# Loads ahead of stores in a step's DMA issues, and four output weights split in place instead of through DRAM

## The chip, the cores and the metric

One core of one Trainium2 chip runs the whole program. The metric is the device time of one execution in microseconds (us), the median of three runs. The profile is one more execution, recorded instruction by instruction.

## What is computed

```python
def _attn_ref(q, k, v, mem_k, mem_v):            # q, k, v: (4, 8, 768, 64)
    chunk, left_ctx, right_ctx = (32, 16, 8)
    for c in range(seq // chunk):                # queries c*32 to c*32+31
        k_full = [mem_k, k[l_start:r_end]]       # 8 memory rows and a local window
        a = softmax(q_c @ k_full.T / sqrt(64))
        out[c] = a @ v_full

def reference(...):
    x = attn_out as 3072 tokens x 512
    x = (sigmoid(x @ w_gate) * (x @ w_val)) @ w_out          # 512 -> 1536 -> 512
    h = x @ w_in                                             # 512 -> 2048
    g = (a0 + a1*h + a2*h**2 + a3*h**3) / (1 + |b0|*|h| + |b1|*h**2 + 1e-6)
    return g @ w_out                                         # 2048 -> 512
```

The first line of each function stands for its shapes; the window arithmetic is shortened. Weights arrive as 64-bit floats and are turned into 32-bit ones on the chip.

## The kernel before, in words

**Precision.** Each matrix operand is held as two parts, a high part (rounded to the type fp32r) and the rest, and each product is three matmuls (high by high, high by low, low by high). So a weight goes through four operations before it can be used. Two ACT passes (`conv_scale`, L309 and L310) and one DVE pass (`conv_bits`, L315) make a 32-bit tile from the 64-bit *stage tile* `st`. One ACT pass (`split_hi`, L344) and one DVE pass (`split_lo`, L348) make the pair of parts from that. A pair is a 128x2x512 tile named `wp` (first layer) or `wpw` (second layer).

**Weights through DRAM.** A pair that is needed again later is written to DRAM (`store_split`, L351, into `wqa`, `wqs` or `w2d`) and read back when needed (`load_split`, L354; `load_w2`, L996 to L1007, for the second layer's output weights in `w2d`). There are 32 units of second-layer weights. `need` lists them in the order in which they are wanted. The input weights of the second layer come first, on the whole, and its output weights last.

**Stages.** Tokens are taken in six blocks `j` of 512. (a) 24 steps, blocks 0 and 1 by 12 hidden tiles `f` (L919 to L935): gate and value products `gate_val` (L372), the sigmoid and its product, the output product `out1` (L574) of the step before, and parts of the attention (scores L112 and L219, the transposes L171 and L264, the products with v L186 and L279). Block 0 also converts the first layer's weights, three units a step. (b) `quads(2, ...)`, 12 steps: blocks 2 and 3 as one pair, with seven products in place of eight (L489). (c) `outs(3, ...)`, 13 steps: output products that are left of block 3, with attention for blocks 4 and 5 between them. (d) `quads(4, ...)`, 12 steps, and `outs(5, ...)`, 13 steps, the same for blocks 4 and 5. (e) The second layer, 6 blocks by 16 tiles (L617, L625 to L645, L656).

**What sets the order.** Nothing is scheduled by a planner. The text's order is each engine's order. A table `plan` holds calls for numbered steps (`at(step, fn, ...)`), and `run(fn, ...)` carries out those of the current step that have one of the names given. So the order of the `run` lines within a step sets the order on every engine. Nearly all transfers are issued by SP, one queue in program order. If one transfer there waits for the engine that makes its data, or for its buffer to come free, everything behind it waits as well. `STORES` (L917) are the writes of weight pairs, `LOADS` (L918) the reads of q, k, v and of stage tiles, and `store1_end` the writes of a finished block of the first layer (`x2d`, L595). Stage tiles and pairs share a pool of 20 buffers; a load waits until what last used its buffer has been read.

Of the kernel before, what the change touches and what calls it, by code (L numbers as in the profile page):

```python
# [22 lines left out]
NF1, NF2 = DFF1 // P, DFF2 // P  # L23
# [14 lines left out]
NPAIR = 8  # L38
PAIRS = ((2, 3), (4, 5))
AHEAD = 4  # L40


@with_exitstack
def fused_kernel(ctx: ExitStack, tc: tile.TileContext, q, k, v, w1, w2, coef, x2d, w2d, wqa, wqs, out):
# [267 lines left out]
    def conv_bits(key, dst):  # L312

        w0, y = words(key)
        nc.vector.scalar_tensor_tensor(  # L315
            out=dst.bitcast(I32), in0=y, scalar=3, in1=w0, op0=ALU.logical_shift_left, op1=ALU.bitwise_or
        )
        del stage[key]
# [20 lines left out]
    def split_tile(key):  # L339
        wp[key] = wpool.tile([P, 2, 512], F32R, tag="w", name="wp" + "_".join(map(str, key)))  # L340
        return wp[key]

    def split_hi(key, src):
        nc.scalar.activation(out=split_tile(key)[:, 0], in_=src, func=ACTF.Copy)  # L344

    def split_lo(key, src):
        t = wp[key]
        nc.vector.tensor_tensor(out=t[:, 1], in0=src, in1=t[:, 0].bitcast(F32), op=ALU.subtract)  # L348
# [4 lines left out]
    def load_split(key, src):  # L353
        nc.sync.dma_start(out=split_tile(key).bitcast(F32), in_=src)  # L354
# [9 lines left out]
    def b_tile(name, dt, shape):  # L364
        return bpool.tile(shape, dt, tag="b", name=name)
# [25 lines left out]
    def gate_val(j, f, m):  # L391
        if (j, f) == (0, 0):
            if m == 0:
                for u in range(2):
                    first[u] = ps(f"h0_0_{u}")
                for h in range(2):
                    for u in range(2):
                        gv_mm(first[u], j, f, u, h)
            gv_out(first[m], j, f, m)
            return  # L400
        pt = ps(f"h{j}_{f}_{m}")
        for h in range(2):
            gv_mm(pt, j, f, m, h)
        gv_out(pt, j, f, m)
# [63 lines left out]
    def quad_key(ja, fp, w):  # L468
        return ("q", ja, fp) + w

    def quad_load(ja, fp, i0=0, n=len(PRODUCTS)):
        for w, _, _ in PRODUCTS[i0 : i0 + n]:
            src = wqa[2 * fp + w[1], w[2]] if w[0] == "a" else wqs[4 * fp + w[1]]
            load_split(quad_key(ja, fp, w), src)

    def quad(ja, fp, m, fill):
# [6 lines left out]
        def product(i):  # L483
# [13 lines left out]
            if m == 1:  # L497
                del wp[quad_key(ja, fp, w)]
                if i < len(PRODUCTS) - AHEAD and fp < NF1 // 2 - 1:
                    quad_load(ja, fp + 1, i + AHEAD, 1)  # L500

# [48 lines left out]
    def g_held(j, f):  # L550
        key = j, f // 4
        if key not in gh:
            p, tag = (xpool, "x") if f < 8 else (bpool, "b")
            gh[key] = p.tile([P, 4, 512], F32, tag=tag, name=f"gh{j}_{f // 4}")
        return gh[key][:, f % 4]

    def g_split(key, sg, n):
        t = gpool.tile([P, 2, 512], F32R, tag="g", name="g" + "_".join(map(str, key)))
        nc.scalar.activation(out=t[:, 0, 0:n], in_=sg, func=ACTF.Copy)  # L559
        nc.vector.tensor_tensor(out=t[:, 1, 0:n], in0=sg, in1=t[:, 0, 0:n].bitcast(F32), op=ALU.subtract)  # L560
        gp[key] = t
# [3 lines left out]
    def out1(j, f, mid=None):  # L565

        if f == 0:
            acc[j] = [accp.tile([P, 512], F32, tag=f"acc{d}", name=f"acc{j}_{d}") for d in range(KT)]
        w, g = wp.pop((1, j, f, 2)), gp.pop((1, j, f))
        for d in range(KT):  # L570
            if d == 2 and mid:
                mid()
            for i, (a, b) in enumerate(TERMS):
                nc.tensor.matmul(  # L574
                    acc[j][d],
                    lhsT=w[:, a, d * P : (d + 1) * P],
                    rhs=g[:, b],
                    start=(f == 0 and i == 0),
                    stop=(f == NF1 - 1 and i == 2),
                )  # L580
        if f == NF1 - 1:
            store1(j)
# [10 lines left out]
    def store1_end():  # L593
        for j, d, s in held:
            nc.sync.dma_start(out=x2d[j, :, d], in_=s)  # L595
        held.clear()
# [126 lines left out]
    c2 = {}  # L723
# [7 lines left out]
    def conv2_bits(i):  # L731
        c2[i] = t2(f"c2_{i}")
        conv_bits(f"2_{i}", c2[i])

    def conv2_hi(i):
        split_hi(("w2", i), c2[i])

    def conv2_lo(i):
        split_lo(("w2", i), c2.pop(i))

    def conv2_store(i):
        store_split(("w2", i), w2d[i])
# [5 lines left out]
    def at(si, *call):  # L748
        plan.setdefault(si, []).append(call)
# [16 lines left out]
    for i in range(2 * NF1):  # L766
        s0 = 10 + i // 2
# [5 lines left out]
    for t in range(4, NPAIR, 2):  # L773
        s0 = 2 if t == 4 else 5
# [31 lines left out]
    S1 = len(steps)  # L806
# [6 lines left out]
    O1 = S1 + NF1  # L813
    Q2 = O1 + NF1 + 1
    O2 = Q2 + NF1
# [7 lines left out]

    need = sorted(range(2 * NF2), key=lambda u: u // 2 + 5 * (u % 2))
    conv_at = [4, 5, 7, 13, 15, 17, 19] + [S1 + 1 + i for i in range(5)] + [O1 + 1 + 3 * i for i in range(4)]
    rest = 2 * NF2 - len(conv_at)
    conv_at += [Q2 + i * 10 // rest for i in range(rest)]
    used = set()
    for u, s0 in zip(need, conv_at):
        at(s0, conv2_load, u, s0 not in used and (S1 <= s0 < O1 or s0 >= Q2))  # L830
        used.add(s0)
        at(s0 + 1, conv2, u)
        at(s0 + 1, conv2_bits, u)
        at(s0 + 2, conv2_hi, u)
        at(s0 + 2, conv2_lo, u)
        at(s0 + 3, conv2_store, u)

    PRE, LAG2 = 3, 5
    with tc.manual_schedule():
# [67 lines left out]
        def runner(si):  # L907
            acts = plan.get(si, [])

            def run(*fns):  # L910
                for fn, *args in acts:
                    if fn in fns:
                        fn(*args)

            return run

        STORES = conv2_store, w_comb_store, w1_store  # L917
        LOADS = load_qk, load_qk2, load_v, conv2_load, load_w1  # L918
        for si, (j, f) in enumerate(steps):  # L919
            run = runner(si)  # L920
            store1_end()
            run(*STORES)
            run(*LOADS)
            run(w1_load, quad_load)
            run(w1_hi, attn_exp, bits1)
            gate_val(j, f, 0)
            run(w1_lo, attn_sum, attn_mul, pv, attn_t, pair_t, w_comb, x_comb)
            gate_val(j, f, 1)
            run(scale1)
            g_split((1, j, f), sgs.pop((j, f)), 512)  # L930
            run(attn_qk, attn_max, conv2_hi, conv2, w_comb_hi, x_comb_hi)
            if si:
                out1(*steps[si - 1], mid=lambda: run(pair_out, pair_qk, pair_max))
            run(pair_sum)
            run(w_comb_lo, x_comb_lo, conv2_lo, conv2_bits)  # L935
# [4 lines left out]
        def load_out(n):  # L940
            nonlocal n_out
            for v in visits[n_out : n_out + n]:
                w1_load(*v, OUT)
            n_out += n

        def visit(run):
            nonlocal nv
            out1(*visits[nv], mid=lambda: run(pair_out, pair_qk, pair_max))
            nv += 1

        def quads(ja, s0, last):
            for i in range(NF1):
# [3 lines left out]
                if m == 0 and fp < NF1 // 2 - 1:  # L956
                    quad_load(ja, fp + 1, 0, AHEAD)
                if i:
# [12 lines left out]
        def outs(j, s0, fn):  # L971
            for i in range(NF1 + 1):
                run = runner(s0 + i)
                load_out(1)
                run(quad_load)
                store1_end()
                run(*STORES)
                run(*LOADS)
                for nxt in visits[nv + 2 : nv + 3]:
                    if nxt[0] == j:  # L980
                        g_split((1, *nxt), g_held(*nxt), 512)
                fn(i)
                run(x_comb, attn_exp)
                run(x_comb_hi, conv2_hi, conv2)
                visit(run)
                run(pair_t)
                run(x_comb_lo, conv2_lo, conv2_bits, pair_sum)

        quads(2, S1, False)
        outs(3, O1, lambda i: None)  # L990
        quads(4, Q2, True)
        nc.scalar.activation(out=cab, in_=cf[:, 4:6], func=ACTF.Abs)
        w2_next, w2t = 0, {}
        in_b = 14

        def load_w2(n):  # L996
            nonlocal w2_next
            for u in need[w2_next : w2_next + n]:
                i = w2_next
                w2_next += 1  # L1000
                if i >= in_b:
                    load_split((2, u), w2d[u])
                    continue
                if i % 2 == 0:
                    w2t[i // 2] = b_tile(f"w2_{i // 2}", F32R, [P, 2, 2, 512])
                wp[2, u] = w2t[i // 2][:, i % 2]
                nc.sync.dma_start(out=wp[2, u].bitcast(F32), in_=w2d[u])  # L1007
# [108 lines left out]
```

## Time and profile before

| | us |
|---|---|
| runs | 1184.07, 1183.54, 1183.27 (median 1183.54) |
| the profiled execution | 1184.93, of which the recorded span is 1183.1 |
| PE (TensorE matmul) busy in the span | 1158.7 (98%) |
| DVE busy | 863.9 (73%) |
| ACT busy | 710.5 (60%) |
| POOL busy | 2.1 |
| mean granted TensorE clock | 0.987 of full speed |

PE is busy 98% of the span, so a time can only fall if its 24.4 us of idle time shrink, if its work shrinks, or if the stretches at a lower clock do. The page's line of granted clock and the tables by stretch show where those are. The `[idle <-engine ...]` behind a row of a timeline gives the idle time of that engine just ahead of the row, and what ended it.

### The profile page before, as it was taken

What the parts mean: (1) busy time and instruction counts of PE and PEld (TensorE: products, weight loads), DVE (VectorE), ACT (ScalarE), POOL (GpSimd) and SP (SyncE); (2) the same over time, 40 slices, a digit from 0 to 9 for tenths busy, and PEclk for the clock granted to TensorE, in tenths of its full rate; (3) what the DMA queues carried; (4) which work ended last, traced back from release to release, by engine and by line L of the source; (5) the groups of instructions that cost most, each with busy time, mean ns of one, the idle gap of its engine ahead of it and who ended that gap; (6) DMA issues with size and microseconds to landing.
All of it is one profiled execution on the core that took longest, in us unless ns stands there. A gap on an engine that the chain in (4) does not pass through costs nothing.

```text
span 1183.1 us, 19935 instructions
## 1 busy us (share of the span) xinstructions
PE 1158.7 (98%) x7942; PEld 953.0 (81%) x7945; DVE 863.9 (73%) x1342; ACT 710.5 (60%) x1208; POOL 2.1 (0%) x15
## 2 busy tenths in 40 slices
PE   7999899999999998999999999999999999999998
PEld 5787688888888887888888888888888888888887
DVE  5677777865576645555662799898888888898885
ACT  4887556653453355344433776767776776767764
POOL 0000000000000000000000000000000000000000
PEclk8899899999999998999999999999999999999999
DMA  8796499997968668988879360100100100100001
GB/s 326 280 372 221 160 371 361 380 391 293 359 243 294 230 226 309 342 337 326 327 287 349 121 244 1 55 18 9 45 19 9 45 19 9 51 12 1 36 1 36
DMA packets 68508, 222.29 MB, mean 188 GB/s; under 512 B 7616, under 2 KB 7872, under 8 KB 68416
## 3 DMA queue, kind: packets, MB, share of 16 engines
q1 hardware_dynamic: 67840, 219.61, 50.2%
q8 instruction: 63, 1.03, 0.3%
q10 hardware_dynamic: 576, 1.41, 0.3%
q14 instruction: 29, 0.24, 0.1%
HBM read 163.32 MB, written 57.67 MB: 187 GB/s over the span
## 4 chain that ended last, share of the span: by engine, by line
PE 87%; DMA 5%; ACT 4%; DVE 3%; SPq 1%; issue 1%
PE acc L656 22%; PE h L617 22%; PE p L489 19%; PE acc L574 13%; PE h L372 7%; DMA st<-w_in 4%; PE xp L279 1%; PE sp L219 1%; DMA k<-k_in 1%; PE xp L186 1%; DVE wp L348 1%; ACT st L309 1%; ACT st L310 1%; PE tp L264 0%; DMA q<-q_in 0%
## 5 line engine op out<-in xcount | busy, mean ns | idle before, releaser
L574 PE MATMUL acc<-g,wp 128*128 128x512 f32 x864 | 212.2, 395 | 0.6 <-ACT x2s L589 0.6
L574 PEld LDWEIGHTS acc<-g,wp 128*128 128x128 f32 x864 | 161.4, 189 | 35.4 <-ACT x2s L589 1.0
L656 PE MATMUL acc<-wp,g 128*128 128x512 f32 x792 | 189.4, 389 | 0.0
L656 PEld LDWEIGHTS acc<-wp,g 128*128 128x128 f32 x792 | 148.7, 188 | 30.9
L625 ACT ACTIVATE t<-h,cf 128x512 f32<-128x512 f32 x96 | 74.8, 779 | 148.4 <-PE h L617 148.4
L617 PE MATMUL h<-x,w 128*128 128x512 f32 x648 | 155.5, 389 | 0.0
L372 PE MATMUL h<-x,wp 128*128 128x512 f32 x576 | 142.0, 401 | 4.7 <-ACT sg L383 3.1
L617 PEld LDWEIGHTS h<-x,w 128*128 128x128 f32 x648 | 121.6, 188 | 25.3
L489 PE MATMUL p<-b,wpq_s 128*128 128x512 f32 x576 | 138.4, 389 | 0.0
L372 PEld LDWEIGHTS h<-x,wp 128*128 128x128 f32 x576 | 110.5, 194 | 29.2 <-ACT sg L383 4.3
L489 PEld LDWEIGHTS p<-b,wpq_s 128*128 128x128 f32 x576 | 108.1, 188 | 22.4
L617 PE MATMUL h<-x,wp 128*128 128x512 f32 x504 | 121.1, 389 | 0.0
L617 PEld LDWEIGHTS h<-x,wp 128*128 128x128 f32 x504 | 94.6, 188 | 19.7
L628 DVE TENSOR_TENSOR t<-t,h 128x512 f32<-128x512 f32 x96 | 65.8, 686 | 55.7 <-ACT hh L627 54.2
L559 ACT ACTIVATE g<-sg 128x512 fp32r<-128x512 f32 x36 | 22.7, 629 | 107.0 <-DVE sg L519 63.7
L656 PE MATMUL acc<-w,g 128*128 128x512 f32 x360 | 86.5, 389 | 0.0
L656 PEld LDWEIGHTS acc<-w,g 128*128 128x128 f32 x360 | 67.6, 188 | 14.0
L629 DVE SCALAR_TENSOR_TENSOR t<-t,cf,h 128x512 f32<-128x512 f32 x96 | 71.8, 748 | 3.4
L489 PE MATMUL p<-x,wpq_a 128*128 128x512 f32 x288 | 73.1, 389 | 0.0
L630 DVE SCALAR_TENSOR_TENSOR qq<-hh,cab,qq 128x512 f32<-128x512 f32 x96 | 71.6, 746 | 0.0
L644 DVE SCALAR_TENSOR_TENSOR t<-t,cf,y 128x512 f32<-128x512 f32 x96 | 71.5, 744 | 0.0
L643 DVE SCALAR_TENSOR_TENSOR qq<-qq,y 128x512 f32<-128x512 f32 x96 | 65.8, 685 | 7.1 <-ACT y L638 7.1
(118 smaller groups left out, 1509.9 us busy)
## 6 DMA issues: line engine op xcount, KB each, us to landing
st<-w_in SPq DMA_DIRECT2D x62, 512.0 KB, 7.4
wp<-wqa SPq DMA_DIRECT2D x60, 512.0 KB, 7.3
wpq_s<-wqs SPq DMA_DIRECT2D x48, 512.0 KB, 8.6
wpq_a<-wqa SPq DMA_DIRECT2D x36, 512.0 KB, 7.9
w2d<-wpw SPq DMA_DIRECT2D x32, 512.0 KB, 6.6
wqa<-wp SPq DMA_DIRECT2D x30, 512.0 KB, 9.3
v<-v_in SPq DMA_DIRECT2D x24, 512.0 KB, 8.7
wqs<-wps SPq DMA_DIRECT2D x24, 512.0 KB, 6.5
```

Of the source, the lines that this page charges most:

```text
L372: nc.tensor.matmul(pt, lhsT=w[:, a, c : c + P], rhs=x[:, kt, b], start=(h == 0 and kt == 0 and i == 0), stop=(h == 1 and kt == 1 and i == 2),)
L489: nc.tensor.matmul(bank[n], lhsT=wt[:, a, c : c + P], rhs=x[:, kt, b], start=(i < 4 and kt == 0 and t == 0), stop=(kt == 1 and t == 2), sk ...
L559: nc.scalar.activation(out=t[:, 0, 0:n], in_=sg, func=ACTF.Copy)
L574: nc.tensor.matmul(acc[j][d], lhsT=w[:, a, d * P : (d + 1) * P], rhs=g[:, b], start=(f == 0 and i == 0), stop=(f == NF1 - 1 and i == 2),)
L617: nc.tensor.matmul(hp, lhsT=w[:, a, kt * P : (kt + 1) * P], rhs=x[kt // 2][:, kt % 2, b], start=(kt == 0 and i == 0), stop=(kt == KT - 1 a ...
L625: nc.scalar.activation(out=t, in_=hp, func=ACTF.Identity, scale=cf[:, 3:4], bias=cf[:, 2:3])
L628: nc.vector.tensor_tensor(out=t, in0=t, in1=hp, op=ALU.mult)
L629: nc.vector.scalar_tensor_tensor(out=t, in0=t, scalar=cf[:, 1:2], in1=hp, op0=ALU.add, op1=ALU.mult)
L630: nc.vector.scalar_tensor_tensor(out=qq, in0=hh, scalar=cab[:, 1:2], in1=qq, op0=ALU.mult, op1=ALU.add)
L643: nc.vector.scalar_tensor_tensor(out=qq, in0=qq, scalar=QC, in1=y, op0=ALU.add, op1=ALU.mult)
L644: nc.vector.scalar_tensor_tensor(out=t, in0=t, scalar=cf[:, 0:1], in1=y, op0=ALU.add, op1=ALU.mult)
L656: nc.tensor.matmul(acc[j][m], lhsT=g[:, a, m * P : (m + 1) * P], rhs=w[:, b], start=(f == 0 and i == 0), stop=(f == NF2 - 1 and i == 2),)
```

## The change

It has two parts. First, in the steps of stage (a), the stage and q, k, v loads are now issued ahead of that step's stores; before, the stores went first. In `outs` the loads move ahead of the stores too, and `store1_end` goes to the end. `quads` keeps its order. Second, of the 32 units of second-layer weights, the last four in `need` (`DIRECT = 4`: units 25, 27, 29 and 31) are no longer written to `w2d` and read back. They are loaded during the last `outs`, at its steps -1, 1, 3 and 5, converted three steps later, and split a step after that straight into the tile that the second layer reads. The twelve before them in `need` are spread over the same ten steps of `quads(4, ...)` that sixteen shared. No matmul is added, removed or moved.

```diff
+DIRECT = 4
...
+    def key2(i):
+        return (2, i) if i in need[2 * NF2 - DIRECT :] else ("w2", i)
+
     def conv2_hi(i):
-        split_hi(("w2", i), c2[i])
+        split_hi(key2(i), c2[i])
 
     def conv2_lo(i):
-        split_lo(("w2", i), c2.pop(i))
+        split_lo(key2(i), c2.pop(i))
...
-    rest = 2 * NF2 - len(conv_at)
+    rest = 2 * NF2 - len(conv_at) - DIRECT
     conv_at += [Q2 + i * 10 // rest for i in range(rest)]
+    conv_at += [O2 + -1 + 2 * i for i in range(DIRECT)]
     used = set()
-    for u, s0 in zip(need, conv_at):
-        at(s0, conv2_load, u, s0 not in used and (S1 <= s0 < O1 or s0 >= Q2))
+    for n, (u, s0) in enumerate(zip(need, conv_at)):
+        lag = 1 if n < 2 * NF2 - DIRECT else 3
+        at(s0, conv2_load, u, s0 not in used and (S1 <= s0 < O1 or Q2 <= s0) and n < 2 * NF2 - DIRECT)
         used.add(s0)
-        at(s0 + 1, conv2, u)
-        at(s0 + 1, conv2_bits, u)
-        at(s0 + 2, conv2_hi, u)
-        at(s0 + 2, conv2_lo, u)
-        at(s0 + 3, conv2_store, u)
+        at(s0 + lag, conv2, u)
+        at(s0 + lag, conv2_bits, u)
+        at(s0 + lag + 1, conv2_hi, u)
+        at(s0 + lag + 1, conv2_lo, u)
+        if n < 2 * NF2 - DIRECT:
+            at(s0 + lag + 2, conv2_store, u)
...
             run = runner(si)
-            store1_end()
-            run(*STORES)
             run(*LOADS)
             run(w1_load, quad_load)
+            run(*STORES)
+            store1_end()
             run(w1_hi, attn_exp, bits1)
...
                 load_out(1)
                 run(quad_load)
+                run(*LOADS)
+                run(*STORES)
                 store1_end()
-                run(*STORES)
-                run(*LOADS)
...
-            for u in need[w2_next : w2_next + n]:
+            for u in need[w2_next : min(w2_next + n, 2 * NF2 - DIRECT)]:
```

The first place where the order of issues matters is SP in steps 8 and 9 of block 0, where the stage tiles of hidden tiles 10 and 11 (`st_10_0` to `st_11_2`) and one of the second layer (`st_4`) are loaded. Before:

```order
58 L351 DMA wqa<-wp_0_7_2_1154 128x1024
59 L351 DMA w2d<-wpw_0_1254 128x1024
60 L300 DMA st_10_0_1275<-w_in 128x512
61 L300 DMA st_10_1_1277<-w_in 128x512
62 L300 DMA st_10_2_1279<-w_in 128x512
63 L300 DMA st_4_1281<-w_in 128x512
64 L351 DMA wqa<-wp_0_8_2_1287 128x1024
65 L351 DMA w2d<-wpw_2_1381 128x1024
66 L300 DMA st_11_0_1398<-w_in 128x512
67 L300 DMA st_11_1_1400<-w_in 128x512
68 L300 DMA st_11_2_1402<-w_in 128x512
```

And now (line numbers are one higher there):

```order
57 L352 DMA wqa<-wp_0_6_2_1030 128x1024
58 L301 DMA st_10_0_1273<-w_in 128x512
59 L301 DMA st_10_1_1275<-w_in 128x512
60 L301 DMA st_10_2_1277<-w_in 128x512
61 L301 DMA st_4_1279<-w_in 128x512
62 L352 DMA wqa<-wp_0_7_2_1154 128x1024
63 L352 DMA w2d<-wpw_0_1254 128x1024
64 L301 DMA st_11_0_1396<-w_in 128x512
65 L301 DMA st_11_1_1398<-w_in 128x512
66 L301 DMA st_11_2_1400<-w_in 128x512
```

The four loads of a step now stand ahead of the two stores of the pairs that DVE finishes in the step before; the store of the step before that is what they now follow.

The second place is SP in steps 3 to 6 of `outs(3, ...)`, with the stage tiles of units 9 and 18 and the stores of units 16 and 9 (`v` and `wp` rows are loads that keep their places). Before:

```order
260 L351 DMA w2d<-wpw_16_4987 128x1024
261 L300 DMA st_9_5074<-w_in 128x512
262 L354 DMA wp_3_8_2_5096<-wqa 128x1024
263 L95 DMA v_5098<-v_in 128x1024
264 L95 DMA v_5100<-v_in 128x1024
265 L354 DMA wp_3_9_2_5140<-wqa 128x1024
266 L354 DMA wp_3_10_2_5237<-wqa 128x1024
267 L351 DMA w2d<-wpw_9_5149 128x1024
268 L300 DMA st_18_5240<-w_in 128x512
```

And now:

```order
260 L301 DMA st_9_5073<-w_in 128x512
261 L352 DMA w2d<-wpw_16_4987 128x1024
262 L355 DMA wp_3_8_2_5096<-wqa 128x1024
263 L96 DMA v_5098<-v_in 128x1024
264 L96 DMA v_5100<-v_in 128x1024
265 L355 DMA wp_3_9_2_5140<-wqa 128x1024
266 L355 DMA wp_3_10_2_5237<-wqa 128x1024
267 L301 DMA st_18_5239<-w_in 128x512
268 L352 DMA w2d<-wpw_9_5149 128x1024
```

Each stage load has changed places with the one store ahead of it.

The third place is ACT in the last `outs(5, ...)`, where `g` rows are the split of the hidden values that `out1` multiplies. What stands there now:

```order
564 L560 ACTIVATE g_5_3_6729<-gh_0_5624 128x512
565 L345 ACTIVATE wp_25_6733<-c_25_6723 128x512
566 L560 ACTIVATE g_5_4_6750<-gh_1_6009 128x512
567 L609 ACTIVATE x_0_0_6753<-x2f_0_6463 128x512
568 L310 ACTIVATE st_27_6668<-st_27_6668 128x512
569 L311 ACTIVATE st_27_6668<-st_27_6668 128x512
570 L560 ACTIVATE g_5_5_6777<-gh_1_6009 128x512
571 L609 ACTIVATE x_0_0_6753<-x2f_1_6465 128x512
572 L345 ACTIVATE wp_27_6783<-c_27_6773 128x512
573 L560 ACTIVATE g_5_6_6798<-gh_1_6009 128x512
574 L609 ACTIVATE x_0_1_6754<-x2f_2_6558 128x512
575 L310 ACTIVATE st_29_6727<-st_29_6727 128x512
```

Before, only the `g` and `x` rows stood here; the L310, L311 and L345 rows are new at this place (they stood in `quads(4, ...)`), each scale pass ahead of the next `g`.

## Rows read from the trace of the kernel before

**Rows 1.** Busy time by stretch (stretch, its length, then each engine; PEclk, DMA share, GB/s).

```profile
core 0: us, PE busy (x) PEld busy (x) DVE busy (x) ACT busy (x) POOL busy (x), PEclk, DMA share, GB/s
120.00:140.00 20.00, 16.24 (x241) 12.67 (x240) 14.89 (x26) 12.03 (x20) 0.00 (x0) 0.83 0.46 177
140.00:420.00 280.00, 280.00 (x2632) 231.42 (x2631) 190.63 (x286) 135.87 (x223) 0.83 (x5) 1.00 0.85 315
460.00:480.00 20.00, 20.00 (x195) 16.93 (x189) 11.10 (x17) 8.76 (x16) 0.00 (x0) 0.83 1.02 399
480.00:1160.00 680.00, 680.00 (x3002) 563.06 (x3001) 538.52 (x816) 430.48 (x730) 0.00 (x0) 1.00 0.31 112
```

**Rows 2.** Timeline of PE, block 0, steps 6 to 11 (start, duration, instruction, idle ahead).

```profile
86.14 3.01 PE L372 MATMUL h<-x,wp 128*128 128x512 f32 x12
...
97.15 1.13 PE L186 MATMUL xp<-at,v 64*64 64x32 f32 x62 [0.88 <-DVE s L145]
...
115.46 3.02 PE L372 MATMUL h<-x,wp 128*128 128x512 f32 x12 [1.28 <-ACT sg L383]
...
123.62 1.47 PE L219 MATMUL sp<-k,q 64*32 64x64 f32 x126 [0.27 <-ACT sg L383]
...
131.09 1.13 PE L186 MATMUL xp<-at,v 64*64 64x32 f32 x62 [1.47 <-DVE s L247]
132.42 1.09 PE L171 MATMUL tp<-ident,s 128*128 128x128 f32 x4 [0.20 <-DVE s L247]
...
135.33 4.75 PE L372 MATMUL h<-x,wp 128*128 128x512 f32 x12 [1.82 <-ACT sg L383]
```

**Rows 3.** Timeline of ACT in the same steps.

```profile
71.80 0.68 ACT L309 ACTIVATE st<-st 128x512 f32<-128x512 f32 x1 [2.47 <-DMA st<-w_in]
...
103.51 0.66 ACT L309 ACTIVATE st<-st 128x512 f32<-128x512 f32 x1 [3.55 <-DMA st<-w_in]
...
107.20 0.68 ACT L309 ACTIVATE st<-st 128x512 f32<-128x512 f32 x1 [1.25 <-DMA st<-w_in]
...
111.05 1.28 ACT L151 ACT_TABLE_LOAD   x1
```

**Rows 4.** Timeline of SP's queue in the same steps (start and length of the issue).

```profile
97.96 0.33 SPq L351 DMA_DIRECT2D w2d<-wpw  x1
98.34 2.60 SPq L300 DMA_DIRECT2D st<-w_in  x4
...
110.73 1.77 SPq L300 DMA_DIRECT2D st<-w_in  x3
```

**Rows 5.** Timeline of PE, steps 5 and 6 of `outs(3, ...)`.

```profile
444.44 2.07 PE L279 MATMUL xp<-at,v 64*64 64x32 f32 x128
...
459.79 3.56 PE L279 MATMUL xp<-at,v 64*64 64x32 f32 x128 [3.94 <-ACT at L266]
463.28 11.42 PE L574 MATMUL acc<-g,wp 128*128 128x512 f32 x42
```

**Rows 6.** Timeline of ACT there.

```profile
458.07 0.65 ACT L309 ACTIVATE st<-st 128x512 f32<-128x512 f32 x1 [2.76 <-DMA st<-w_in]
...
459.16 1.06 ACT L266 ACTIVATE at<-tp 128x512 f32<-128x512 f32 x2
```

**Rows 7.** Timeline of SP's queue there.

```profile
437.69 1.59 SPq L354 DMA_DIRECT2D wp<-wqa  x2
452.23 0.32 SPq L351 DMA_DIRECT2D w2d<-wpw  x1
452.64 0.38 SPq L300 DMA_DIRECT2D st<-w_in  x1
```

**Rows 8.** Timeline of PE in the last `outs(5, ...)`.

```profile
615.97 30.08 PE L574 MATMUL acc<-g,wp 128*128 128x512 f32 x132
```

**Rows 9.** Timeline of SP's queue there.

```profile
622.98 2.36 SPq L595 DMA_DIRECT2D x2d<-x2s  x4
```

**Rows 10.** The page's part on DMA issues (count, KB each, median us to landing).

```profile
st<-w_in SPq DMA_DIRECT2D x62, 512.0 KB, 7.4
```

## The prediction

> **What bounds the kernel now.** I read the table of busy time by stretch first. PE is busy 98% of the span, so a gain must come from the few stretches where it is not, or where its clock is down. From 140 to 420 us and from 480 to 1160 us PE is busy 100% at clock 1.00, whatever ACT, DVE and the DMA engines do [rows 1]. There, nothing that this change moves can gain; it can only lose. Of the 24.4 us of idle time about 10 lie at two places that the edit touches: late in block 0 (85 to 140 us), and around 456 to 460 us. The rest lies at the start and the end of the program, which it does not reach.
>
> The second reading is PE's timeline at these places, for the idle time ahead of each row and its releaser. In block 0 there are gaps of 0.88, 1.28, 0.27, 1.47, 0.20 and 1.82 us, 5.92 in all, each ended by ACT or DVE [rows 2]. In `outs(3)` there is one, of 3.94 us, ended by ACT's transposed copy `at` (L266) [rows 5].
>
> The third is ACT's timeline, for what made ACT late. It waits 2.47, 3.55 and 1.25 us for stage tiles in block 0 [rows 3] and 2.76 us for one in `outs(3)`, with the `at` copy right behind it [rows 6]. The engine named in PE's row is thus not the cause; a stage load is.
>
> The fourth is SP's queue, for why the load was late. At 97.96 a store of a split pair is issued, and 0.38 us later the four stage loads behind it; the next step's stage loads go out at 110.73 in the same way [rows 4]. In `outs(3)` SP's last issue ends at 439.28, then the queue stands for 13 us until the pair of the store exists (452.23), and the stage load follows at 452.64 [rows 7]. It lands some 5.4 us later, when ACT's row begins [rows 6]. So loads are late because a store at the head of the queue waits for DVE.
>
> **The change, part by part.** *Loads ahead of stores, block 0.* The four loads that were issued at 98.34 now stand behind the store of one step earlier. What gates them then is their buffers: PE's products of step 6 and bit passes of DVE of about that time. PE's row ends at 89.15 [rows 2], so they go out near 90, and with a median of 7.4 us to landing [rows 10] are there near 98. ACT wants them at 99.96 (103.51 less the wait of 3.55 [rows 3]). The wait goes, with about 2 us to spare. The next group goes out from about 98 to 102 in place of 110.73. ACT's 1.25 at 107.20 goes as well. ACT's rows run without a break from there up to its table load at 111.05 [rows 3] and the sigmoid behind it, which ended PE's 1.28 at 115.46. ACT was late by 3.55 + 1.25 = 4.80, more than the 1.28 that PE lost, so this gap goes whole. The gaps of 0.88, 0.27, 1.47 and 0.20 hang on the same lateness through ACT and DVE in order, the first one on the wait at 71.80. I count them as gone: 4.10 for the five.
>
> The last gap, 1.82 at 135.33, has another part. The sigmoid stands behind two table loads of 1.28 each [rows 3] around an exponential that needs a maximum from DVE. Bounds are 0 and 1.82; I take 1.4, since the lateness goes but the table loads stay.
>
> *The clock.* The granted clock is 0.83 over 120 to 140 us and again over 460 to 480 us [rows 1], and 1.00 in the stretches between. 1.00 is the level of 2.4 GHz, and means between 0.5 and 1 mix it with 1.2. Both drops come right behind the largest gaps. Twelve products at 135.33 took 4.75 against 3.01 usual: 1.74 lost [rows 2]. After the 3.94 gap, 128 small products took 3.56 against 2.07: 1.49. Then 42 output products took 11.42, where 30.08 / 132 x 42 = 9.57 is usual: 1.85 [rows 5, 8]. Together 5.1. The gap of 1.28 at 115.46 was followed by products of 3.02, no loss [rows 2]. So if at most a gap of that size stays, the clock should stay up, and I count all 5.1.
>
> A rule of the Trainium skill speaks against this: "TensorE: Matmul & The Clock Gate", Part 1, says that the cost of warming up varies from run to run and is under 1% of a typical span, so one should not fit to it. By that rule the clock terms would be left out, and the saving would be 9.4. Here they are 0.4% of the span, and the three runs lie within 0.07% of each other, so in this kernel the loss seems to recur at the same place; I keep them.
>
> *Loads ahead of stores, `outs(3)`.* The load that went out at 452.64 now stands ahead of the store that waited, and follows the issues that ended at 439.28 [rows 7]. It lands near 447, some 8 us before ACT asks for it at 455.3 (458.07 less 2.76 [rows 6]). ACT's two scale passes then end by 456.4, and `at` (1.06 for both [rows 6]) is ready for PE at about 457 at the latest, where it was at 459.8. PE stood from 455.85 [rows 5]. Since the stage tile of unit 9, three steps before, also comes sooner, ACT gets ahead by more than that last wait, and I count the 3.94 whole.
>
> *Later stores.* A store is now issued behind a step's loads, which stand only for buffers. From 140 us on there are no stage loads of the first layer in the queue, and PE has no gap [rows 1]. The buffers that the stores hold are wanted by ACT some microseconds later at the tightest place I find (step 8), about the time of landing. I put 0 there; bounds 0 and 1, covered by ACT's idle time.
>
> *Four weights in place.* Four stores and four reads of 512 KB go, from stretches where PE is full, so they gain nothing. In `quads(4)` four conversions fewer gain nothing either. In the last `outs` each conversion adds two scale passes of 0.65 (the L309 row of [rows 6]) and one split pass, about 1.9 us, to ACT and two passes to DVE, ahead of the next split of hidden values `g`. PE works there 30.08 us without a gap on 132 products, 2.73 us for the 12 of one hidden tile [rows 8]. ACT's own work per tile is one or two passes of some 0.6, so per two tiles 2.4 + 1.9 of 5.46: the passes fit. What might not fit is the landing. Unit 29's load stands behind the `x2d` writes that SP issues only at 622.98 [rows 9]. I estimate that it goes out near 626.5, lands by 634 at the median, or by 637 behind the other loads there, and that ACT, one tile each 2.73 us, reaches it at about 633.6. The hidden split behind it would be ready by 639.5, and PE, at its pace, wants it at about 643. So I put 0. Below, the bound is 0, since PE has nothing to gain there. Above, if the landing is 4 us later still for two units, it is 2 x 4 and a clock drop of 3.3.
>
> **Sum.** Gaps 4.10 + 1.4 + 3.94 = 9.4, clock 5.1, together 14.5. The profiled execution of 1184.9 would become 1170.4. It stood 1.4 above the median of its runs (1183.5), so the median would be 1169.0.
>
> **The rivals.**
> - *One place only.* The waits in `outs(3)` go (3.94 + 3.34 = 7.3), but in block 0 the loads land no sooner, because the loads merely collide earlier with those of q, k and v. For it: a load needs 7.4 us at the median [rows 10], and early loads share the engines. Against: ACT's waits end 5 to 9 us after the issue [rows 3, 4], so the queue made them late. 1183.5 - 7.3 = 1176.2. The mirror case gives about the same.
> - *The clock does not come back.* Gaps go but a remaining one of 1 to 2 us still drops the clock in both places: 1183.5 - 9.4 = 1174.1. This is also what the rule on the clock gate above would forecast. Against: the drops followed only gaps that were long or close together.
> - *Slower: the in-place conversions stall the last `outs`.* ACT works in order, and the scale pass of a late stage tile would stand ahead of each `g`. For it: the queue is blocked for the `x2d` writes until 622.98 [rows 9] and the DMA engines are full behind it. It begins to cost when a landing is over 3.7 us later than I think. One stalled unit costs about 4 and a clock drop of 3.3. To end slower than before, all four must stall, 4 x (4 + 1) = 20 against 14.5, so 1189. Against: only two of them are issued behind the writes.
> - *Nothing moves.* The buffers of the early loads come free no earlier than the stores' data, and SP stands for the buffer in the place of the store: 1183.5. Against: PE's products that free them end at 89.15, 9 us ahead of the old issue [rows 2, 4].
>
> **How the numbers follow.** Something under 0.2% (2.4 us) can't be told from no change here. The forecast case has 0.70, one place only 0.10, the clock case 0.08, nothing moves 0.06, slower 0.06. The forecast's own bounds are 1167.5 (1.82 whole, and small losses of block 0 that I did not count) and 1171.5 (0.88 and all of 1.82 stay). The range takes in the clock case and one place only: 1167 to 1176.5. Faster has 0.70 + 0.10 + 0.08 = 0.88, the others 0.06 each.
>
> **What would show it.** In the new profile ACT has no wait for a stage tile over 0.5 us between 60 and 480 us; SP issues the four loads near 90 and the one of `outs(3)` before 445; PE's rows have no idle time over 1.3 us from 85 to 480 us; the granted clock is 1.00 in all stretches from 40 us on; the last `outs` has no gap. It is wrong if PE has a new wait for ACT behind 600 us, if a gap stays with ACT no longer waiting for DMA, or if the clock drops behind a small gap.

## The result, and the profile after

| | us | |
|---|---|---|
| before | 1183.80 | median of 4 runs, 1183.27 to 1185.47 |
| after | 1170.32 | median of 4 runs, 1169.01 to 1171.62 |
| ratio | 0.9884 | 95% interval 0.9866 to 0.9902 |

The change saves 13.5 us, 1.2%. It was forecast at 1169.0 us with a range of 1167.0 to 1176.5. In the profiled executions the span fell from 1183.1 to 1169.7 us, by 13.4. PE's busy time fell by 5.3 of these (1158.7 to 1153.4), and its idle time by 8.1.

The table of busy time by stretch of the kernel after answers to [rows 1]:

```profile
core 0: us, PE busy (x) PEld busy (x) DVE busy (x) ACT busy (x) POOL busy (x), PEclk, DMA share, GB/s
...
80.00:100.00 20.00, 20.00 (x211) 16.23 (x211) 16.73 (x31) 18.19 (x36) 0.19 (x1) 1.00 0.71 256
100.00:120.00 20.00, 20.00 (x271) 16.31 (x271) 15.18 (x28) 15.74 (x28) 0.00 (x0) 1.00 0.66 261
120.00:140.00 20.00, 19.36 (x203) 15.64 (x204) 16.77 (x28) 11.66 (x21) 0.00 (x0) 1.00 0.66 218
140.00:420.00 280.00, 278.24 (x2676) 229.51 (x2674) 183.82 (x274) 135.20 (x221) 0.83 (x5) 0.99 0.83 307
440.00:460.00 20.00, 19.44 (x209) 16.03 (x208) 13.59 (x21) 11.70 (x22) 0.00 (x0) 1.00 0.76 278
460.00:480.00 20.00, 20.00 (x90) 16.45 (x89) 8.22 (x13) 7.84 (x14) 0.00 (x0) 1.00 1.01 389
600.00:650.00 50.00, 50.00 (x223) 41.40 (x222) 26.66 (x42) 27.21 (x47) 0.00 (x0) 1.00 0.71 268
```

Late block 0 PE is now full but for 0.64 us, and the clock stays at 1.00 both there and after 460 us. But the stretch from 140 to 420 us, which was full before, now lacks 1.76 us, and its clock is 0.99. PE's own timeline shows both, and answers to [rows 2, 5]. The releaser "issue" means that the profile shows nothing that PE waited for:

```profile
126.57 3.02 PE L373 MATMUL h<-x,wp 128*128 128x512 f32 x12 [0.64 <-ACT sg L384]
129.43 2.88 PE L575 MATMUL acc<-g,wp 128*128 128x512 f32 x12
...
207.09 1.25 PE L220 MATMUL sp<-k,q 64*32 64x64 f32 x102
210.10 0.44 PE L220 MATMUL sp<-k,q 64*32 64x64 f32 x26 [1.76 <-issue]
210.47 2.16 PE L575 MATMUL acc<-g,wp 128*128 128x512 f32 x6
212.43 4.03 PE L373 MATMUL h<-x,wp 128*128 128x512 f32 x12
...
420.76 3.02 PE L575 MATMUL acc<-g,wp 128*128 128x512 f32 x12 [0.58 <-ACT x2s L590]
...
447.04 1.64 PE L575 MATMUL acc<-g,wp 128*128 128x512 f32 x6
...
451.06 0.48 PE L280 MATMUL xp<-at,v 64*64 64x32 f32 x18 [0.50 <-issue]
451.47 9.81 PE L575 MATMUL acc<-g,wp 128*128 128x512 f32 x42
461.12 1.52 PE L490 MATMUL p<-x,wpq_a 128*128 128x512 f32 x6
```

Since PE's order is the same in both kernels, the same instruction can be looked up in both. These are the rows of the kernel before:

```profile
139.92 2.91 PE L574 MATMUL acc<-g,wp 128*128 128x512 f32 x12
...
427.76 3.02 PE L574 MATMUL acc<-g,wp 128*128 128x512 f32 x12 [0.60 <-ACT x2s L589]
...
454.21 1.64 PE L574 MATMUL acc<-g,wp 128*128 128x512 f32 x6
...
474.53 1.52 PE L489 MATMUL p<-x,wpq_a 128*128 128x512 f32 x6
```

The products at 86.14 [rows 2] start at 85.20 after, so the start of the program is 0.94 ahead. Those at 139.92 start at 129.43, 10.49 ahead: block 0 gave 9.55. Those at 427.76 start at 420.76, only 7.00 ahead: 3.49 was lost between, around 208 us. From 454.21 to 474.53 the lead grows from 7.17 to 13.41: `outs(3)` gave 6.24. After that it stays at 13.4 to the end. So this is where the time came from, and where part of it went.

SP's queue shows the mechanism, in answer to [rows 4, 7]:

```profile
86.87 2.18 SPq L301 DMA_DIRECT2D st<-w_in  x4
...
94.17 0.33 SPq L352 DMA_DIRECT2D w2d<-wpw  x1
94.59 2.06 SPq L301 DMA_DIRECT2D st<-w_in  x3
...
431.44 0.38 SPq L301 DMA_DIRECT2D st<-w_in  x1
444.00 0.32 SPq L352 DMA_DIRECT2D w2d<-wpw  x1
```

The four stage loads go out at 86.87 (98.34 before) and the one of `outs(3)` at 431.44 (452.64 before). There the store behind it still waits 12 us for its pair; now nothing urgent stands behind it. ACT has no wait for a stage tile any more in either place: its timeline from 40 to 170 us has no row ended by a stage load, and from there to 460 us there is none either. One comes right behind `outs(3)`: 2.87 us at 461.87, in a stretch where PE is full (460 to 480 us in the table).

### The profile page after: what moved, and what is told of

Read it like the earlier page. It is cut to its first block, busy times and chain, and to the rows that moved or that the text cites. A ratio compares the mean times of both kernels' runs of the same rounds, so it can differ in the third digit from the quotient of the medians.

```text
span 1169.7 us, 19955 instructions
## 1 busy us (share of the span) xinstructions
PE 1153.4 (99%) x7945; PEld 948.6 (81%) x7945; DVE 865.2 (74%) x1342; ACT 709.0 (61%) x1208; POOL 2.1 (0%) x15
## 4 chain that ended last, share of the span: by engine, by line
PE 93%; ACT 3%; DMA 2%; DVE 2%; issue 1%; SPq 0%; ACTq 0%
PE acc L657 22%; PE h L618 22%; PE p L490 20%; PE acc L575 15%; PE h L373 10%; PE xp L280 1%; DMA st<-w_in 1%; PE sp L220 1%; PE xp L187 1%; PE tp L265 0%; DMA q<-q_in 0%; ACT st L310 0%; ACT st L311 0%; PE sp L113 0%; DVE x L292 0%
```

## The experiments

The theory: stage loads were late because a store whose data did not exist yet stood at the head of SP's queue; PE's gaps, and the lower clock behind them, followed from that. The four weights in place are worth nothing. The first four kernels take the change apart.

**e1_steps**: only the steps of blocks 0 and 1.

```diff
-DIRECT = 4
+DIRECT = 0
...
+                store1_end()
+                run(*STORES)
                 run(*LOADS)
-                run(*STORES)
-                store1_end()
```

> Only the reordering in the 24 steps of blocks 0 and 1; outs as before, all 32 weights through DRAM. Theory (a store at the head of SP's queue held the stage loads): PE's gaps of 85 to 140 us and the clock loss behind them go, by the two traces 8.9 us, and 1.2 us at the start; the 3.94 us gap of outs(3) and its slow products stay. 1183.8 - 10.1 = 1173.7 us, or up to 3.6 more in executions in which PE stands without a releaser near 210 us. Rival (the in-place weights are what frees SP and the DMA engines): under 3 us gained, 1181 or more.

Measured: 1176.61 us (ratio 0.9941, 0.9926 to 0.9956), 6.8 gained: inside the range for the theory, but 3.3 short of the 10.1 forecast. In `outs(3)` the gap stayed, and was longer (4.68 us); ACT waits there for the stage tile:

```profile
449.49 0.65 ACT L310 ACTIVATE st<-st 128x512 f32<-128x512 f32 x1 [3.46 <-DMA st<-w_in]
```

Near 208 us PE stood for 0.94 us, with "issue" as releaser. These two, 0.74 and 0.94, are 1.7 of the 3.3 us that are missing.

**e2_outs**: only `outs`.

```diff
-DIRECT = 4
+DIRECT = 0
...
+            store1_end()
+            run(*STORES)
             run(*LOADS)
             run(w1_load, quad_load)
-            run(*STORES)
-            store1_end()
```

> Only the reordering in outs; steps as before, all 32 weights through DRAM. Theory: only the 3.94 us gap and the slow products behind it go, 6.6 to 7.3 us: 1176.5 to 1177.2 us; block 0 keeps its gaps of 5.9 us. Rival (the gap in outs(3) is fed by lateness from block 0, or by the weights): under 3 us gained, 1181 or more.

Measured: 1177.79 us (0.9954, 0.9941 to 0.9967), 5.7 gained, nearly a microsecond less than expected. The gap of `outs(3)` is gone whole, and block 0 keeps its gaps:

```profile
134.63 4.81 PE L373 MATMUL h<-x,wp 128*128 128x512 f32 x12 [1.82 <-ACT sg L384]
...
455.05 2.07 PE L280 MATMUL xp<-at,v 64*64 64x32 f32 x128
457.04 9.81 PE L575 MATMUL acc<-g,wp 128*128 128x512 f32 x42
...
473.19 1.66 PE L490 MATMUL p<-x,wpq_a 128*128 128x512 f32 x6 [0.89 <-ACT p L526]
```

The last row has a new gap of 0.89, early in the quads, for ACT; it is about as long as what is missing, but no run shows that it is the reason. So the two places are separate. Each gives somewhat less alone than was forecast, together 12.5 us, where both orders at once gain 13.7 (`e3_order`, next).

**e3_order** (`DIRECT = 0`, all else as changed) and **e4_direct** (`DIRECT = 4`, both orders as before):

> Both reorderings, all 32 weights through DRAM. Theory: the four in-place weights are worth 0, so this stands at the changed kernel's time, 1169.0 to 1171.5 us. Rival (the in-place weights carry part of the gain): 1173 us or more. Rival (they cost something in the last outs): below 1168.5 us.

> Only the four weights in place, both orders as before. Theory: PE is busy 100% in all stretches that this touches, so no change, 1183 to 1185 us, and no PE gap in the last outs. Rival (fewer transfers ahead of Q2 or in it free the queue): 1181 us or less. Rival (scale passes wait for stage tiles behind the stores and stall g): 1187 us or more.

Measured: e3_order 1169.74 us (0.9884, 0.9869 to 0.9899), the same ratio as the change itself; e4_direct 1183.88 us (1.0001, 0.9990 to 1.0012). So the whole gain is the order of issues, and the weights in place neither help nor harm. The 0.9990 to 1.0012 is the closest that this study comes to showing a zero.

**after_again, e5_block0, e6_quads.** The three kernels so far with the new order in the steps (the kernel after, e1_steps, e3_order) all had the stand of PE near 208 us, a halt inside a group of products with "issue" as releaser; the kernel before, e2_outs and e4_direct did not. In e5_block0 only block 0 (`j == 0`) issues loads first; e6_quads reorders `quads` as well.

```diff
+            if j:
+                store1_end()
+                run(*STORES)
             run(*LOADS)
             run(w1_load, quad_load)
-            run(*STORES)
-            store1_end()
+            if not j:
+                run(*STORES)
+                store1_end()
```

> The changed kernel once more, unaltered. It shows how the stand of PE near 208 us (1.76 us in the first profile, no releaser named) varies, and what it does to the time. If it is in every execution at the same instruction but of another length, it belongs to the program: 1169 to 1171.6 us. Rival (a chance event of one execution): no such gap in this profile.

> The change, but only the steps of block 0 issue loads first; the steps of block 1 keep stores first. Theory on the stand of PE near 208 us: PE waits there for its own next instructions, whose transfer stands behind data that the new order of issues in block 1 piles up; with the old order there the transfer comes some 6 us ahead of need as in the kernel before, the gap goes, and the gains at the two places stay: 1167 to 1168.5 us. Rival (the pile is there because PE runs 10 us earlier against the same DMA work, whatever the order): the gap stays, 1169 to 1171.6 us. Rival (block 1's order carries part of the gain): 1172 us or more.

> The change, and the same reordering in quads as well (loads, then stores, then store1_end). Theory: PE is busy 100% in both quads, so there is nothing to gain: the time of the changed kernel, 1169 to 1171.6 us; the only PE gap near (0.58 us, behind the eviction of block 2) is ACT's and stays. Rival (loads in quads also come late and lag into outs): 1168 us or less.

Measured: after_again 1170.08 us (1169.24 to 1170.64), e5_block0 1168.28 (1168.16 to 1169.04), e6_quads 1170.73 (1169.05 to 1172.36). PE near 208 us in after_again, and then in e5_block0:

```profile
207.09 1.25 PE L220 MATMUL sp<-k,q 64*32 64x64 f32 x102
209.56 0.44 PE L220 MATMUL sp<-k,q 64*32 64x64 f32 x26 [1.22 <-issue]
209.93 1.65 PE L575 MATMUL acc<-g,wp 128*128 128x512 f32 x6
211.42 2.89 PE L373 MATMUL h<-x,wp 128*128 128x512 f32 x12
```

```profile
206.88 1.48 PE L220 MATMUL sp<-k,q 64*32 64x64 f32 x128
208.29 1.65 PE L575 MATMUL acc<-g,wp 128*128 128x512 f32 x6
```

The stand belongs to the program: it is behind the 102nd of 128 score products in five profiles (0.94, 1.22, 1.22, 1.22 and 1.76 us). With the old order in block 1 it is gone, and the median falls by 1.8 us. That is little, and the intervals of the two ratios overlap (0.9852 to 0.9883 and 0.9865 to 0.9901), but the four runs of each do not. e6_quads shows no gain from `quads`, as argued.

What PE waited for there is read from the part on DMA queues. The whole kernel after has

```profile
q8 instruction: 62, 1.02, 0.4%
```

62 transfers of 16 KB against 7945 products and as many weight loads on PE: some 256 of PE's instructions to a transfer, if they are PE's. The Trainium skill ("Runtime: NRT & Kernel Launch", Terms) says that an engine's instruction memory is a FIFO refilled in blocks of 16 KiB, which agrees with these 16 KB. The transfer next to the stand begins in the kernel after between 207.4 and 207.6 us, as the part on queues of that window shows:

```profile
q8 instruction: 1, 0.02, 31.7%
```

PE's 102nd product ends at 208.34. In the kernel before, the corresponding transfer is in the window of 212 to 213 us, and PE comes to the 102nd product near 218.7, some 6 us later; in e5_block0 it is in the window of 201 to 202, against 208. In the five profiles with the stand, the transfer begins between 207.0 and 207.9 us, and PE goes on 2.2 to 2.5 us after that each time.

**e8_shift, e9_pile.** Two tests of that reading.

```diff
-        idle_mm(12)
+        idle_mm(24, 256)
```

```diff
         store_split(("s", i), wqs[i])
+        if 12 <= i < 16:
+            store_split(("s", i), wqs[i])
```

> The change, with the 12 idle products of 512 columns at the start written as 24 of 256, so that every later instruction of PE stands 12 products further back in its stream, at the same work. Theory (PE waits near 208 us for a block of its own instructions): blocks have a fixed count of instructions, so the stand moves 12 products ahead in the same group of 128 score products, from behind the 102nd to behind the 90th, again 0.9 to 1.8 us; time 1169 to 1171.6 us. Rival (PE waits there for a buffer or for operands of the 103rd product): the stand stays behind the 102nd.

> The kernel in which only block 0 issues loads first, with four stores of 512 KB of combined weights (steps 17 and 18 of 24) issued twice, some 5 us more of transfers at full rate ahead of PE's stand. Theory (the block of instructions stands behind piled-up data): the stand comes back behind the 102nd score product near 207 us, 0.5 us or more, or, if the block is still just in time, its transfer begins 2 us or more nearer to that product than the 6 us of the kernel without the extra stores. Rival (the order of issues in block 1 itself makes the stand): no stand, and the transfer of the block stays some 6 us ahead.

e8_shift is the kernel after with 12 more products at the start; its time was 1168.11 us (0.9874, 0.9858 to 0.9891). The stand near 208 us neither moved to the 90th product, as the theory had it, nor stayed behind the 102nd, as the rival had it: it was gone, and the block's transfer came at 201 to 202 us. PE comes to that group at 207.17 us (207.09 in the kernel after) under the same order of issues, so this speaks against a wait for operands or buffers of the 103rd product. The other stand without a releaser, at the start of every profile, did move by just 12 products: from behind the 58th of 64 (row of the kernel after) to behind the 46th (row of e8_shift).

```profile
20.78 0.43 PE L187 MATMUL xp<-at,v 64*64 64x32 f32 x6 [1.98 <-issue]
```

```profile
17.59 0.90 PE L187 MATMUL xp<-at,v 64*64 64x32 f32 x46 [1.46 <-ACT at L174]
20.48 0.80 PE L187 MATMUL xp<-at,v 64*64 64x32 f32 x18 [1.99 <-issue]
```

A third stand shows the same in mid-kernel: among the small products of `outs(3)` it lies behind the 110th of 128 in the kernel after, e5_block0 and e9_pile, and behind the 98th in e11_both (below), which has the 12 more products:

```profile
445.38 1.70 PE L280 MATMUL xp<-at,v 64*64 64x32 f32 x98
447.99 0.66 PE L280 MATMUL xp<-at,v 64*64 64x32 f32 x30 [0.92 <-issue]
```

So these stands lie at a fixed count of PE's instructions. e9_pile missed its aim. The second store to the same place waited for the first to land (SP waited 7.7 us there for its own stores), so no data piled up; SP's queue stood instead. Its rows, and PE's:

```profile
194.62 9.33 SPq L352 DMA_DIRECT2D wqs<-wps  x4
203.99 0.43 SPq L203 DMA_DIRECT2D q<-q_in  x1
204.51 1.28 SPq L206 DMA_DIRECT2D k<-k_in  x2
```

```profile
209.87 0.96 PE L220 MATMUL sp<-k,q 64*32 64x64 f32 x64 [2.67 <-DMA k<-k_in]
211.54 1.06 PE L220 MATMUL sp<-k,q 64*32 64x64 f32 x64 [0.71 <-DMA k<-k_in]
233.24 2.90 PE L577 MATMUL acc<-g,wp 128*128 128x512 f32 x6 [3.32 <-DMA wp<-wqa]
```

It took 1178.86 us (0.9965, 0.9949 to 0.9980), 10.6 more than e5_block0. By accident it shows the main theory plainly: a waiting store put ahead of loads that were in time makes them late (`q` goes out at 203.99, at 196.22 in e5_block0), and PE stands for them, in a place that was full.

**e10_pile2, e11_both.** The piling done properly, into DRAM that nothing else uses (for the steps before the stand), and the two remedies together.

```diff
+        if 10 <= i < 14:
+            store_split(("s", i), pile[i - 10])
```

> The kernel in which only block 0 issues loads first, with the stores of combined weights of two steps (near 185 and 194 us) written a second time to a place in DRAM that nothing else uses: 2 MB more ahead of PE's stand, with no wait on the first copy. It computes the same output. Theory (PE's block of instructions is delayed by piled-up data): the transfers of the two blocks, at 194 and 201 us without the extra stores, come 2 us or more later, and PE stands again behind the 102nd score product near 207 us with no releaser named, or gets the block under 4 us ahead. Rival (the order of issues in block 1, not the amount, decides): the blocks still come at 194 and 201. If q and k come late instead, PE's row names their DMA.

> Only block 0 issues loads first, outs as changed, four weights in place, and the idle products as 24 of 256 columns: the two variants without the stand near 207 us put together. Theory: both take away the same 1.4 to 3.6 us, so together no more than either: 1167 to 1168.5 us. Rival (each takes away something of its own): below 1166.5 us.

e10_pile2: 1169.18 us (1168.63 to 1171.60). The two blocks came in the windows of 197 to 198 and 203 to 204 us, 2 to 3 us later on the clock of the profile, but PE itself ran 1.0 us later (the products at 126.41 in e5_block0 start here at 127.41). The second block was still over 5 us ahead, and PE did not stand. So the theory's main expectation was missed: 2 MB more of data delayed the blocks by 1 to 2 us, not by the 6 of the kernel after. The rival, that only the order counts and the blocks come as before, does not fit whole either. e11_both: 1168.15 us (1167.96 to 1168.53), no better than either remedy alone, as expected: they remove the same stand.

What stays open is why the block's transfer is late in the new order of block 1. That it is late, and that PE stands for it, is read from the count of instructions and from the times of the transfers; no run shows it directly. That full DMA engines delay it is only argued: e8_shift had them as full (share 1.00 to 1.03 from 190 to 210 us), and its block was in time.

## Why the prediction was right, and where its sizes were off

The sign, the two places, the chain from store to stage load to ACT to PE, and the zero for the weights in place were as predicted, each shown by a kernel of its own. SP issued the loads at 86.87 and 431.44 ("near 90", "before 445"). The remaining gap behind the two table loads was forecast at 0.4 us and measured 0.64. In the last `outs` ACT did wait, 1.05 and 1.20 us, for the last two stage tiles, and PE did not, as the slack of some 3.7 us allowed:

```profile
621.40 0.67 ACT L310 ACTIVATE st<-st 128x512 f32<-128x512 f32 x1 [1.05 <-DMA st<-w_in]
...
626.47 0.67 ACT L310 ACTIVATE st<-st 128x512 f32<-128x512 f32 x1 [1.20 <-DMA st<-w_in]
```

The sum was 14.5 and the profiled executions differ by 13.4. That these are so close is in part luck: block 0 gave 2.3 more than forecast and the start 0.9, `outs(3)` gave 1.0 less, and block 1 took 3.5. Three of the signs that were named did not come: PE had a gap over 1.3 us (the 1.76 near 208 us), the clock was not 1.00 in all stretches (0.99), and ACT waited for a stage tile over 0.5 us (the 2.87 at 461.87, at no cost to PE). Term by term:

- **Block 0**: forecast 4.10 + 1.4 + 1.74 = 7.2, measured 9.55. The idle time that went was as forecast (6.20 in the stretches from 80 to 140 us to 0.64, 5.56 against 5.5). The term that was mis-sized is the slower work: 4.0 in place of 1.74. Of it 2.2 ran at the lower clock: the row at 135.33, and the transposes at 132.42 (1.09 for four [rows 2], 0.66 in the kernel after), which I had left out. The other 1.8 lies in rows beside the smaller gaps, at a clock of 1.00, and I had no term for it. Half of that is in three groups of products that a gap cuts in two, such as the 2 and 62 products around the gap of 0.88: 0.30 and 1.13 us, where 64 in one piece take 1.14 in the kernel after.
- **The clock in block 0**: I had it fall behind the gap of 1.82, before the products at 135.33. It had fallen by 133 us, ahead of that gap (133.51 to 135.33) and behind those of 1.47 and 0.20. The stretches of the kernel before show it (PEclk is the third number from the end):

```profile
132.00:133.00 1.00, 0.80 (x17) 0.72 (x10) 1.00 (x3) 0.97 (x2) 0.00 (x0) 0.63 0.06 16
133.00:134.00 1.00, 0.51 (x3) 0.10 (x1) 1.00 (x3) 0.98 (x2) 0.00 (x0) 0.50 0.31 123
```

- **`outs(3)`**: forecast 3.94 + 3.34 = 7.3, measured 6.24. The whole gap went, but 0.50 us came in its place in the group of small products, of the same kind as the stand near 208 us.
- **Block 1**: forecast 0, with the words that there is nothing to gain there and only something to lose. It lost 3.49, and the step that failed is "from 140 us on there are no stage loads of the first layer in the queue, and PE has no gap ... I put 0 there; bounds 0 and 1". I looked for buffers and ACT, not for PE's instructions. The loss of 3.49 is 1.76 of idle time and the slow products behind it (4.03 for the 12 at 212.43, 2.16 for the 6 at 210.47); after_again, with 1.22, shows none of them. That fits the two pairs among the runs of the kernel after, near 1169.1 and 1171.5 us.
- **The start** gave 0.94, forecast 0. It is chance: 48 products there took 13.94 us in the profile before and 12.57 after, but also 12.92 in e4_direct, with the old order, and 13.89 in e3_order, with the new one.

At the start, 48 products at a mixed clock took anything from 12.57 to 13.94 us. The rule of the Trainium skill ("TensorE: Matmul & The Clock Gate", Part 1), that the cost of warming up varies and should not be fitted, agrees with that. In the two places it does not hold: every profile that had the gaps had the slow products with them, and without the gaps went 2.2 us of work at the lower clock in block 0 (1.74 counted) and some 2.8 of slower work in `outs(3)` (3.34 counted). By the rule's sum, 9.4, the median would have been 1174.1; measured was 1170.3.

## What to carry to other kernels

In a queue that issues in program order, put what is ready ahead of what still waits for an engine: here the early stores gained nothing, and a load behind one was late by the whole wait (13 us in `outs(3)`). Follow a gap of the bounding engine back past the engine that its row names, to that engine's own wait and to the issue of the transfer. Apply such a reordering only where the trace shows a wait: where PE was already full (block 1), the same edit cost 1.8 us by the medians, though nothing where the count of PE's instructions had moved (1168.11 with it in e8_shift, 1168.15 without it in e11_both).

## What had not been expected

- PE can stand in mid-kernel, by all signs for its own instructions. A group of 128 small products, each with a weight load, is 256 instructions, as many as a block, and takes 1.5 us. Where the next block came late, as it seems, PE stood 0.5 to 2.1 us with "issue" as releaser: at the start of every profile, near 208 us in five, and in the small products of `outs(3)` in five (0.50 to 1.68).
- The clock fell behind some gaps and not behind others. It stayed at 1.00 behind 0.64, 0.94, 1.22, 1.28, 1.42 and 1.48 us, and fell behind 1.76 us near 208 us, behind 1.68 us near 450 us in e6_quads, behind 1.47 with 0.20 close after it in block 0, and behind 3.94 and 4.68. So half a microsecond more of a gap near 208 us (1.22 to 1.76) cost 2 us in all.
